# Ten of sixteen blocks of the first feed-forward by seven block products, and a list scheduler behind attention

## The chip, the cores and the metric

The kernel runs on one core of a Trainium2 chip. The metric is device time in microseconds of one execution; smaller is better. A profile is taken of one execution, and its own time is given beside the median of the runs.

## What is computed

Attention over 2 batches of 768 tokens with 8 heads of 64 (a band of near keys and 24 block summaries) gives `x` of 1536 tokens x 512. Then two feed-forwards follow, one behind the other:

```python
h = x @ w_in                      # 512 x 2048
y = (h - tanh(h)) @ w_out         # 2048 x 512
yn = y / sqrt(mean(y * y) + 1e-6) * rms_g
out = (silu(yn @ w_gate) * (yn @ w_val)) @ w_out2   # 512 x 1536 twice, 1536 x 512
```

The inputs are float32. Every operand of a feed-forward product is held as a high and a low part in the reduced format that TensorE multiplies at full rate, and one product is three matmuls: high x high, low x high, high x low.

## The kernel before

**Tiling.** The 1536 tokens are four groups of 384 (three tiles of 128); two groups are a half, `tp`. The columns of `w_in` come in 16 blocks of 128. One step of the first feed-forward (`steps`, L490 to L496) takes one block for one group: `up_mul` (L512) issues 4 x 3 matmuls of 384 columns into a PSUM bank `h`, ScalarE takes the tanh (L528), VectorE subtracts (L531), ScalarE and VectorE make the high and the low part (L536, L540), and three steps later (`LAG`) `down_mul` (L546) multiplies them with the block of `w_out`, nine matmuls of 512 columns. The blocks are done in four bundles (`NCH = [4, 3, 5, 4]`). Within a bundle the products of a token tile stay in one PSUM bank and are then copied or added to `part[t]` (`evac`, L561), so there are 4 x 12 evacuations.

**The second feed-forward** uses block products with fewer multiplications. For 256 columns of weight (`p`), half of the tokens, and the two halves of the 512 rows, the product is a 2 x 2 block product; `unit2` (L649) does it by seven products of sums and differences of blocks (Winograd's form of Strassen's method) instead of eight. A product is 2 x 3 matmuls of 384 columns (`product`, L639). The sums of weight blocks are made on GpSimd in `pair_of` (L225), those of token blocks in `operand` (L627). Intermediate sums build up in three banks `acc`, one `accx` and two `h`. `down2` (L713) then makes six token tiles, each in one of two banks `t2`, and VectorE adds each to `part`.

**The joint.** When a token group has its last part of the first feed-forward, `norm` (L593) takes squares, the inverse root and the scaling; `turn` (L614) transposes the scaled rows on TensorE; `operand` makes the parts.

**Weights** come as words of 64 bits, 512 KB a piece, through two or three buffers `raw`; ScalarE makes the signed part (L190), VectorE shifts and joins (L196, L197), and `split` (L200) makes the high part on ScalarE (L202) and the low part on GpSimd (L205). They lie in 13 slots used in a ring.

**Order.** Attention, with the first nine to twelve steps of the first feed-forward beside it, is issued in an order written out in `ORDER`, under a manual schedule. What stands behind it is issued in program order, with counters of rough time (`adv`, L792, `at`, L778) that say where decoding, norm and operands are put in, and the framework's own scheduler then orders the instructions of each engine by a simulated timeline.

Of the kernel before, what the change touches and what calls it, by code (L numbers as in the profile page):

```python
# [22 lines left out]
GT = 3  # L23
# [5 lines left out]
NCH = [4, 3, 5, 4]  # L29
NG = NT // GW  # L30
G0 = ((0, 3), (3, 3), (6, 3), (9, 3))
GN = tuple((GT * g, GT) for g in range(NG))
NP = FF2 // 256
SLOTS_A = 10
# [7 lines left out]
SB = 13  # L42
# [3 lines left out]
TS0 = 6  # L46
UF = 2
DT0 = 3.5
DT1 = 2.5
DLD = 10  # L50
DTR = 6
DPV = 10
DVL = 10
DEC = (1.8, 1.9)
TP0 = 1.2
TP1 = 1.0
TC = 0.6
TK01 = 1
TV = 4
TK1 = -8  # L60
TV1 = -8
TD0 = 11
DTD = 3.5
TM0 = 28
REST = 38
DM0 = 4
S2 = 2
EV = 4
PSV = 0
PTV = 0  # L70
KBUF = 4
PVS = (1, 1)
PB = 4
PTB = 3
SHIFT = {}
ALT = ()
OSA = 6
SSH = 8
TSEL = 0.3
TQ = (0.2, 3)  # L80
TVL = (6, 16)
ORD = [0, 2, 1, 3]
TKB = (4, 6)
VE = ((0, 1, 0, 0), (1, 1, 1, 1))
DTV = 0.25
# [25 lines left out]
TVS = 10  # L111
TCKW = {"schedule_with_timeline_sim": True}


@with_exitstack
def attn_moe_kernel(ctx: ExitStack, tc: tile.TileContext, ins, out, dbg=None):
# [39 lines left out]
    jobs = []  # L156
    m0 = 0
    for nch in NCH:
        jobs += [(name, m) for name in ("w_in", "w_out") for m in range(m0, m0 + nch)]
        m0 += nch  # L160
    for p in range(NP):
        jobs += [("w_gate", p), ("w_val", p), ("w_out2", 2 * p), ("w_out2", 2 * p + 1)]
    SLOTS_OF = {"w_in": 1, "w_out": 1, "w_gate": 4, "w_val": 3, "w_out2": 1}
    b2 = 2 * sum(NCH[:-2])
    b3 = b2 + 2 * NCH[-2]
    LENT = jobs[b2:b2 + 6] + jobs[b3 + NCH[-1]:b3 + NCH[-1] + 3]
    wt = {}
    nxt = {"job": 0, "slot": 0, "piece": 0}
# [8 lines left out]
    def room(n):  # L177
        while nxt["slot"] + n > free["n"]:
            yield "blocked"

    free = {"n": SLOTS_A, "t": 0.0, "gen": None, "at": 0.0}

    def load(name, m):
        raw = (state["raw"] if "raw" in state else rawp).tile([128, 1024], U32, name="raw")
        nc.sync.dma_start(out=raw, in_=ins[name][m].bitcast(U32))
        return raw.rearrange("p (n t) -> p n t", t=2)
# [5 lines left out]
    def words(r):  # L192
        a = dp.tile([128, 512], F32, name="da")
        t = dt_.tile([128, 512], U32, name="dt")
        signed(a, r)
        V.tensor_scalar(t, r[:, :, 0], 29, None, ALU.logical_shift_right)  # L196
        V.scalar_tensor_tensor(t, a.bitcast(U32), 3, t, ALU.logical_shift_left, ALU.bitwise_or)  # L197
        return t.bitcast(F32)

    def split(hi, lo, d, eng):  # L200
        if eng is A:
            A.activation(hi, d, AF.Copy)  # L202
        else:
            eng.tensor_copy(hi, d)
        G.tensor_tensor(lo, d, f(hi), ALU.subtract)  # L205

    def one(name, m):
        i = nxt["piece"]
        nxt["piece"] += 1
        r = load(name, m)  # L210
        yield
        d = words(r)
        yield
        if (name, m) in LENT:
            k = LENT.index((name, m))
            if k % 3 == 0:
                state["wx"] = state["xp"].tile([128, GT, 2, KD, 128], F32R, name="x2").rearrange("p a b c d -> p a b (c d)")
            w = state["wx"][:, k % 3]
        else:
            yield from room(1)  # L220
            w = slot()
        split(w[:, 0], w[:, 1], d, V if (i < EV) != (f"ev{i}" in ALT) else A)
        wt[name, m] = w

    def pair_of(name, p):  # L225
        r = load(name, 2 * p)
        yield
        d1 = words(r)
        r = load(name, 2 * p + 1)
        yield  # L230
        yield from room(1)
        wa = slot()
        split(wa[:, 0], wa[:, 1], d1, A)
        yield
        d2 = words(r)
        yield
        a11, a12, a21, a22 = d1[:, 0:256], d1[:, 256:512], d2[:, 0:256], d2[:, 256:512]
        sf = state["sf"].tile([128, 4, 256], F32, name="sf")
        G.tensor_tensor(sf[:, 0], a21, a22, ALU.add)
        G.tensor_tensor(sf[:, 1], sf[:, 0], a11, ALU.subtract)  # L240
        G.tensor_tensor(sf[:, 2], a11, a21, ALU.subtract)
        G.tensor_tensor(sf[:, 3], a12, sf[:, 1], ALU.subtract)
        yield from room(2)
        wb, wc = (slot().rearrange("p h (q c) -> p h q c", q=2) for _ in range(2))
        yield
        split(wb[:, 0, 0], wb[:, 1, 0], a22, A)
        yield
        split(wb[:, 0, 1], wb[:, 1, 1], sf[:, 0], A)
        yield
        split(wc[:, 0], wc[:, 1], sf[:, 1:3], A)  # L250
        if name == "w_gate":
            yield from room(1)
            wt["s4", p] = slot().rearrange("p h (q c) -> p h q c", q=2)
        q4 = 0 if name == "w_gate" else 1
        wd = wt["s4", p]
        split(wd[:, 0, q4], wd[:, 1, q4], sf[:, 3], A)
        wa = wa.rearrange("p h (q c) -> p h q c", q=2)
        wt[name, p] = {1: wa[:, :, 0], 2: wa[:, :, 1], 3: wd[:, :, q4], 4: wb[:, :, 0], 5: wb[:, :, 1], 6: wc[:, :, 0], 7: wc[:, :, 1]}

    def decode(name, m):  # L260
        return (pair_of if name in ("w_gate", "w_val") else one)(name, m)

    dec = {}

    def w_load(i):
        dec[i] = {"r": load(*jobs[i])}
        nxt["job"] = i + 1
        nxt["piece"] = i + 1
# [34 lines left out]
    kwin, kmax, vsum, vt_, last = {}, {}, {}, {}, {}  # L303
# [186 lines left out]
    steps = []  # L490
    m0 = 0
    for j, nch in enumerate(NCH):
        for g in GN if j else G0:
            for m in range(m0, m0 + nch):
                steps.append((j, g, m, m == m0, m == m0 + nch - 1))
        m0 += nch  # L496
    acc, part, gs = {}, {}, {}

    def triple(o, wh, wl, xh, xl, start, stop, **kw):
        T.matmul(o, wh, xh, start=start, stop=False, **kw)  # L500
        T.matmul(o, wl, xh, start=False, stop=False, **kw)  # L501
        last["PE"] = T.matmul(o, wh, xl, start=False, stop=stop, **kw)  # L502

    def down(o, w, g, j, first, end):
        js = slice(j * 128, (j + 1) * 128)
        T.matmul(o, g[:, 0, js], w[:, 0], start=first, stop=False)  # L506
        T.matmul(o, g[:, 1, js], w[:, 0], start=False, stop=False)  # L507
        last["PE"] = T.matmul(o, g[:, 0, js], w[:, 1], start=False, stop=end)  # L508
# [3 lines left out]
    def up_mul(i):  # L512
        _, g, m, _, _ = steps[i]
# [11 lines left out]
    def up_tanh(i):  # L525
        h, n = up_h[i]
        t = up_t[i] = tmp()[:, 0:n]
        A.activation(t, h, AF.Tanh)  # L528
# [4 lines left out]
    def up_high(i):  # L533
        t = up_t[i]
        gg = gs[i] = gp.tile([128, 2, GW], F32R, name="g")[:, :, 0:t.shape[-1]]
        last["ACT"] = A.activation(gg[:, 0], t, AF.Copy)  # L536

    def up_low(i):
        gg = gs[i]
        last["DVE"] = V.tensor_tensor(gg[:, 1], up_t.pop(i), f(gg[:, 0]), ALU.subtract)  # L540

    def up_step(i):
        for piece in (up_mul, up_tanh, up_less, up_high, up_low):
            piece(i)

    def down_mul(i, t):  # L546
        j, g, m, first, end = steps[i]
# [6 lines left out]
    def down_step(i):  # L554
        j, g, m, first, end = steps[i]
        for t in range(g[0], g[0] + g[1]):
            down_mul(i, t)
            if end:
                evac(acc.pop(t), t, j == 0)

    def evac(a, t, first, act=False):  # L561
        if first:
            part[t] = pp.tile([128, DM], F32, name="part") if t < 6 else state["pp"].tile([128, DM], F32, name="part2")
            if act or t % 3 == 1:
                A.activation(part[t], a, AF.Copy)  # L565
            else:
                V.tensor_copy(part[t], a)
        else:
            V.tensor_tensor(part[t], a, part[t], ALU.add)  # L569

    def squares(g, v):
        for j in range(GT):
            jk = state["jk"].tile([128, 512], mybir.dt.bfloat16, name="jk")
            A.activation(jk, part[g * GT + j], AF.Square, scale=DM ** -0.5, accum_out=v[:, j:j + 1])

    def inverse(g, v, y):
        r = sp.tile([128, GT], F32, name="rt")
        V.tensor_scalar(v, v, 1e-6, None, ALU.add)
        V.tensor_scalar(r.bitcast(U32), v.bitcast(U32), 1, None, ALU.logical_shift_right)
        V.tensor_scalar(y.bitcast(I32), r.bitcast(I32), -1.0, float(0x5F3759DF), ALU.mult, ALU.add)  # L580
        for _ in range(3):
            V.scalar_tensor_tensor(r, y, -0.5, y, ALU.mult, ALU.mult)
            V.tensor_tensor(r, r, v, ALU.mult)
            V.scalar_tensor_tensor(y, r, 1.5, y, ALU.add, ALU.mult)

    def scaled(g, y, j):
        x = part[g * GT + j]
        if SCE[g][j]:
            A.activation(x, x, AF.Copy, scale=y[:, j:j + 1])
        else:  # L590
            V.tensor_scalar(x, x, y[:, j:j + 1], None, ALU.mult)

# [364 lines left out]
```

## Time and profile before

| What | us |
|---|---|
| median of 3 runs (lowest, highest) | 635.87 (635.28, 636.94) |
| the profiled execution | 637.51 |
| its span, first to last instruction | 635.6 |
| TensorE busy in the span | 610.5 (96%) |
| VectorE | 392.3 (62%) |
| ScalarE | 324.0 (51%) |
| GpSimd | 227.1 (36%) |

Busy times are the union of an engine's instructions. Matmuls are pipelined, so each lasts about twice the distance from one to the next; distances from start to start are what they cost. "PEclk" is the clock granted to TensorE as a share of its full 2.4 GHz. Engines are named PE (TensorE), DVE (VectorE), ACT (ScalarE), POOL (GpSimd) and SP (the queue that issues DMAs); L and a number is a line of the kernel.

### The profile page before, as it was taken

To read this page: it belongs to the slowest core of one execution; us is meant where nothing else is said; L and a number is where in the kernel's file an instruction comes from. 1 tells how busy PE (TensorE), PEld (TensorE's weight loads), DVE (VectorE), ACT (ScalarE), POOL (GpSimd) and SP (SyncE) were. 2 spreads that over 40 slices of the span, in tenths; PEclk is the share of its full clock that TensorE was granted. 3 is DMA by queue.
4 is the path that set the end of the run, shared out by engine and by line. 5 is a ranking of instruction groups with operands and counts; after the bars stand their busy time and mean duration, and the time that the engine had idled before them with its cause. 6 is when DMAs were issued, how large, how long until landed. Compare 5 with 4: busy or idle time off the path is not lost.

```text
span 635.6 us, 9649 instructions
## 1 busy us (share of the span) xinstructions
PE 610.5 (96%) x3528; PEld 556.8 (88%) x3528; DVE 392.3 (62%) x897; ACT 324.0 (51%) x798; POOL 227.1 (36%) x237
## 2 busy tenths in 40 slices
PE   3889999999999999999999889999999999999997
PEld 3779988898989899999998879999999999999995
DVE  3788672455657545545568694765657656657544
ACT  1996984444444444434546575644454363453420
POOL 0666831122222222540000145663555355365300
PEclk9899999999999999999999899999999999999999
DMA  8898710312223222201000020301212122121013
GB/s 331 265 342 244 240 53 26 133 67 100 100 100 121 78 100 100 88 15 65 0 1 1 34 67 1 131 36 66 68 67 72 61 94 72 45 90 34 1 66 133
DMA packets 19640, 58.91 MB, mean 93 GB/s; under 512 B 2168, under 2 KB 5496, under 8 KB 19592
## 3 DMA queue, kind: packets, MB, share of 16 engines
q1 hardware_dynamic: 19592, 58.29, 27.0%
q8 instruction: 28, 0.46, 0.3%
q14 instruction: 20, 0.16, 0.1%
HBM read 54.84 MB, written 3.15 MB: 91 GB/s over the span
## 4 chain that ended last, share of the span: by engine, by line
PE 87%; ACT 5%; DMA 3%; DVE 3%; POOL 1%; issue 1%; SPq 0%; POOLq 0%
PE h L502 8%; PE h L500 8%; PE h L501 8%; PE acc L506 7%; PE acc L508 7%; PE acc L507 7%; PE t L506 5%; PE t L507 5%; PE t L508 5%; PE acc L500 5%; PE acc L502 5%; PE acc L501 5%; PE accx L502 3%; PE accx L501 3%; PE accx L500 3%; ACT P L441 2%
## 5 line engine op out<-in xcount | busy, mean ns | idle before, releaser
L205 POOL TENSOR_TENSOR w<-dt,w 128x512 fp32r<-128x512 f32 (+1 forms) x51 | 63.6, 1247 | 143.9 <-ACT w L202 113.5
L528 ACT ACTIVATE s<-h 128x384 f32<-128x384 f32 x64 | 31.2, 489 | 85.8 <-PE h L502 85.7
L531 DVE TENSOR_TENSOR s<-h,s 128x384 f32<-128x384 f32 x64 | 35.5, 555 | 63.4 <-ACT s L528 62.8
L569 DVE TENSOR_TENSOR part<-t,part 128x512 f32<-128x512 f32 x60 | 40.8, 688 | 41.4 <-PE t L508 40.9
L506 PE MATMUL t<-w,g 128*128 128x512 f32 x144 | 54.8, 395 | 2.8 <-ACT part L565 2.5
L507 PE MATMUL t<-w,g 128*128 128x512 f32 x144 | 56.9, 395 | 0.3 <-DVE g L659 0.3
L506 PE MATMUL acc<-w,g 128*128 128x512 f32 x144 | 57.1, 401 | 0.0
L508 PE MATMUL acc<-w,g 128*128 128x512 f32 x144 | 56.9, 395 | 0.0
L508 PE MATMUL t<-w,g 128*128 128x512 f32 x144 | 56.7, 394 | 0.0
L507 PE MATMUL acc<-w,g 128*128 128x512 f32 x144 | 56.7, 394 | 0.0
L540 DVE TENSOR_TENSOR g<-s,g 128x384 fp32r<-128x384 f32 x64 | 40.8, 640 | 24.0 <-ACT g L536 23.9
L197 DVE SCALAR_TENSOR_TENSOR dt<-da,dt 128x512 uint32<-128x512 uint32 x60 | 50.7, 846 | 5.8 <-ACT da L190 2.8
L501 PE MATMUL h<-x,w 128*128 128x384 f32 x148 | 50.1, 338 | 0.0
L500 PE MATMUL h<-x,w 128*128 128x384 f32 x148 | 49.8, 337 | 0.0
L502 PE MATMUL h<-x,w 128*128 128x384 f32 x148 | 49.7, 337 | 0.0
L658 ACT ACTIVATE g<-s 128x384 fp32r<-128x384 f32 x48 | 24.6, 520 | 49.3 <-POOL s L701 39.2
L536 ACT ACTIVATE g<-s 128x384 fp32r<-128x384 f32 x64 | 33.4, 523 | 30.5 <-DVE s L531 29.9
L659 DVE TENSOR_TENSOR g<-s,g 128x384 fp32r<-128x384 f32 x48 | 31.5, 667 | 24.1 <-ACT g L658 23.8
L190 ACT ACTIVATE da<-raw 128x512 f32<-128x512 f32 x68 | 44.7, 659 | 1.4 <-DMA raw<-w_out 1.3
L441 ACT ACTIVATE P<-P,nb 128x120 f32<-128x120 f32 x96 | 36.5, 384 | 15.3 <-DVE nb L435 15.1
L681 POOL TENSOR_TENSOR s<-s 128x384 f32<-128x384 f32 x12 | 12.2, 1019 | 88.0 <-DVE s L680 88.0
L500 PE MATMUL acc<-x,w 128*128 128x384 f32 x120 | 41.1, 343 | 1.5 <-ACT s L663 1.4
(164 smaller groups left out, 1703.8 us busy)
## 6 DMA issues: line engine op xcount, KB each, us to landing
raw<-w_out SPq DMA_DIRECT2D x28, 512.0 KB, 3.2
raw<-w_in SPq DMA_DIRECT2D x16, 512.0 KB, 4.9
q<-q SPq DMA_DIRECT2D x12, 512.0 KB, 8.9
raw<-w_gate SPq DMA_DIRECT2D x12, 512.0 KB, 3.2
raw<-w_val SPq DMA_DIRECT2D x12, 512.0 KB, 3.1
kw<-kw SPq DMA_DIRECT2D x8, 576.0 KB, 4.5
v<-vw SPq DMA_DIRECT2D x12, 384.0 KB, 5.0
out_dram<-part SPq DMA_DIRECT2D x12, 256.0 KB, 2.0
```

The costliest lines, as they stand in the source:

```text
L190: A.activation(a, r[:, :, 1].bitcast(F32), AF.Prelu, scale=2.0 ** -112, alpha=-(2.0 ** 32))
L197: V.scalar_tensor_tensor(t, a.bitcast(U32), 3, t, ALU.logical_shift_left, ALU.bitwise_or)
L205: G.tensor_tensor(lo, d, f(hi), ALU.subtract)
L441: A.activation(P[:, k], P[:, k], AF.Exp, scale=-1.0, bias=nb[:, k:k + 1], accum_out=sm[:, k:k + 1])
L500: T.matmul(o, wh, xh, start=start, stop=False, **kw)
L501: T.matmul(o, wl, xh, start=False, stop=False, **kw)
L502: last["PE"] = T.matmul(o, wh, xl, start=False, stop=stop, **kw)
L506: T.matmul(o, g[:, 0, js], w[:, 0], start=first, stop=False)
L507: T.matmul(o, g[:, 1, js], w[:, 0], start=False, stop=False)
L508: last["PE"] = T.matmul(o, g[:, 0, js], w[:, 1], start=False, stop=end)
L540: last["DVE"] = V.tensor_tensor(gg[:, 1], up_t.pop(i), f(gg[:, 0]), ALU.subtract)
L569: V.tensor_tensor(part[t], a, part[t], ALU.add)
```

## The change

Six blocks of `w_in` stay in the old form: four in `ORDER` and behind it, and two more, in two bundles. The other ten are five pairs of 256 columns, each done by `unit1`, seven products for each half of the tokens, in the order of `RUNS` (one pair for both halves; then two pairs for the first half and for the second, twice). Their weights are decoded by `pair_of`, now for `w_in` too, and need four slots a pair. The token operands are built from attention's output: `first_sum` adds high and low part, `operand` subtracts and splits; three of the seven use the old tiles as they are, one is written in place, three lie in new tiles. Each unit's six token tiles are multiplied with `w_out` by `down2` during the next unit, over two blocks each, and added to `part` on VectorE. `norm` and the transposes of the joint stand between units at written places. The load of the Silu table (`si`) is issued inside `ORDER`.

All work behind `ORDER` is first recorded as steps with an engine, a cost (time on the engine, latency, and whether it takes the access that VectorE and GpSimd share) and its readers and writers. `Plan.order` gives each step a due time, backwards from TensorE's written order, and places steps one by one, on each engine the one that can start first and, among equals, is due first. `Plan.issue` then issues everything in that order under the manual schedule. TensorE keeps the written order. In `unit2` the first two value products of block 0 come before the fifth gate product, and temporary tiles come from two pools (5 and 8 tiles) in place of one of 13.

```diff
-NCH = [4, 3, 5, 4]
+NCH0 = 4
+NCH1 = 2
+N0 = (NCH0 + NCH1) // 2
+NF = FF1 // 256 - N0
+RUNS = (1, 2, 2)
+FSG = ((0, 0), (1, 1))
+TNE = (('DVE', 'ACT'), ('ACT', 'DVE'))
+START = {"PE": 0.0, "DVE": 1.6, "ACT": 0.0, "POOL": -12.0, "SP": -1.0}
+C_T3, C_D3, C_TURN = (0.524, 0.69, 0), (0.695, 0.86, 0), (0.36, 0.52, 0)
+C_SIGN, C_SHIFT, C_JOIN = (0.56, 0.66, 0), (0.335, 0.416, 1), (0.6, 0.69, 1)
+C_G512, C_G256, C_G384, C_V384 = (1.25, 1.3, 1), (0.67, 0.72, 1), (0.98, 1.02, 1), (0.467, 0.551, 1)
+C_P384, C_P384A, C_E512, C_E512A = (0.467, 0.55, 0), (0.39, 0.49, 0), (0.6, 0.69, 0), (0.48, 0.58, 0)
...
+    def order(self, free):
...
+        while len(start) < len(S):
+            best = None
+            for e, L in line.items():
+                if e == "PE":
+                    L = [i for i in L if at < len(pe) and i == pe[at]]
+                for i in L:
+                    s = max(free[e], ready[i], lock if S[i][1][2] else -1e9)
+                    k = (s, due[i], i)
+                    if best is None or k < best[0]:
+                        best = k, i
...
+            start[i], done[i] = s, s + lat
+            free[e] = s + occ
+            if locks:
+                lock = s + occ
...
+    ctx.enter_context(tc.manual_schedule())
+    for key in ORDER:
+        tasks[key]()
...
+    def unit1(p, tp, fill, odd):
+        w = wt["w_in2", p]
+        ga, gb, gc = (Buf(q) for q in (("accx", "h", "h") if odd else ("acc",) * 3))
...
+        def shrink(s, row, half, ps=None):
+            t, x = Buf("s"), ps or s
+            v = lambda: x.tile[:, 0:GW]
+            act(AF.Tanh, lambda: t.tile, v, [x], [t])
+            if ps:
+                both("DVE", C_P384, lambda: t.tile, v, lambda: t.tile, ALU.subtract, [x], [t])
+            else:
+                both("POOL", C_G384, lambda: t.tile, v, lambda: t.tile, ALU.subtract, [x], [t])
+            g[row, half] = widen(t)
+
+        product(ga, w, tp, 1, True)
+        s11 = taken(ga)
+        product(gb, w, tp, 2, True)
+        added(s11, gb)
+        product(gc, w, tp, 5, True)
+        s22 = taken(gc)
+        product(ga, w, tp, 6, False)
+        s12 = taken(ga)
+        shrink(s11, 0, 0)
+        fill(0)
+        product(ga, w, tp, 7, False)
+        added(s22, ga)
+        shrink(s22, 1, 1)
+        fill(1)
+        product(gc, w, tp, 3, False)
+        added(s12, gc)
+        shrink(s12, 0, 1)
+        fill(2)
+        product(ga, w, tp, 4, False)
+        shrink(None, 1, 0, ga)
+        fill(3)
+        return g
...
+    def first_sum(tp, kk, kh, half):
+        d = xs[tp, kk, kh, half] = Buf("xs")
+        r, x = plain(tp, half, kh, kk)
+        eng = "POOL" if (kh, half) in FSG else "DVE"
+        both(eng, C_G384 if eng == "POOL" else C_V384, lambda: d.tile.rearrange("p (t n) -> p t n", t=GT), lambda: f(x(0)), lambda: f(x(1)), ALU.add, r, [d])
...
+    units, p0 = [], N0
+    for n in RUNS:
+        units += [("w_out", p, tp) for tp in range(2) for p in range(p0, p0 + n)]
+        p0 += n
+    units += [("w_out2", p, tp) for p in range(NP) for tp in range(2)]
+    last_p = N0 + NF - 1
...
+    for n, (name, p, tp) in enumerate(units):
+        if (name, p, tp) == ("w_out2", 0, 1):
+            turned(1, 1)
+            downs(prev, range(6))
+            prev = None
+
+        def fill(k, prev=prev):
+            if n == 0:
+                if k < 3:
+                    down_step(rest[k])
+            elif prev is None:
+                pass
+            elif prev[:2] == ("w_out", last_p):
+                if prev[2]:
+                    if k == 0:
+                        downs(prev, range(6))
+                    elif k == 1:
+                        turned(1, 0)
+                elif k < 2:
+                    downs(prev, range(3 * k, 3 * k + 3))
+            elif k < 3:
+                downs(prev, range(2 * k, 2 * k + 2))
+            if (name, p, tp) == ("w_out", last_p, 1) and k >= TAT:
+                turned(0, k - TAT)
...
+    plan.issue(dict(START))
```

In the diff, `taken` is a copy from PSUM on ScalarE, `added` an addition from PSUM on VectorE, `widen` the high part on ScalarE and the low part on VectorE, `both` an instruction with two inputs, and `turned` the four transposes of a token group, their copies and the operands made of them.

## Rows read from the trace of the kernel before

**Rows 1.** Busy time by stretches: engines, granted clock, DMA share.
```profile
core 0: us, PE busy (x) PEld busy (x) DVE busy (x) ACT busy (x) POOL busy (x), PEclk, DMA share, GB/s
116.70:349.50 232.80, 232.80 (x1179) 210.77 (x1179) 139.64 (x283) 108.98 (x219) 50.52 (x43) 1.00 0.21 73
349.50:384.00 34.50, 29.52 (x151) 26.34 (x150) 25.32 (x48) 22.11 (x48) 11.78 (x10) 0.95 0.13 47
384.00:624.00 240.00, 240.00 (x1250) 223.29 (x1248) 148.63 (x244) 111.83 (x241) 113.34 (x116) 1.00 0.18 62
...
340.00:360.00 20.00, 17.93 (x91) 16.53 (x90) 14.81 (x47) 13.08 (x28) 1.02 (x1) 0.91 0.01 2
```

**Rows 2.** Order in time, TensorE, first feed-forward: start, duration, line, tiles.
```profile
206.38 0.39 PE L506 MATMUL acc<-w,g 128*128 128x512 f32 x1
...
208.46 0.34 PE L500 MATMUL h<-xf,x 128*128 128x384 f32 x1
...
210.58 0.39 PE L506 MATMUL acc<-w,g 128*128 128x512 f32 x1
```

**Rows 3.** Order in time, TensorE, the joint; brackets: idle before, releaser.
```profile
349.48 0.83 PE L619 MATMUL t<-sel,part 128*128 128x128 f32 x6
...
353.47 0.54 PE L500 MATMUL acc<-x,w 128*128 128x384 f32 x1 [1.42 <-ACT s L663]
...
357.24 0.34 PE L500 MATMUL acc<-xf,w 128*128 128x384 f32 x1
...
364.45 0.82 PE L619 MATMUL t<-sel,part 128*128 128x128 f32 x6
365.02 0.42 PE L502 MATMUL h<-x,w 128*128 128x384 f32 x1
...
378.76 0.34 PE L501 MATMUL h<-x,w 128*128 128x384 f32 x1
381.63 0.50 PE L506 MATMUL t<-w,g 128*128 128x512 f32 x1 [2.52 <-ACT part L565]
```

**Rows 4.** Order in time, ScalarE, the joint: table load, first square, last scalings.
```profile
344.69 1.28 ACT L856 ACT_TABLE_LOAD   x1
...
346.10 0.61 ACT L574 ACTIVATE jk<-part 128x512 bf16<-128x512 f32 x1
...
351.32 1.32 ACT L589 ACTIVATE part<-part,ry 128x512 f32<-128x512 f32 x2
```

**Rows 5.** Groups by line and shape: count, busy us, mean ns, idle before.
```profile
L205 POOL TENSOR_TENSOR w<-dt,w 128x512 fp32r<-128x512 f32 x39 | 52.8, 1354 | 141.3 <-ACT w L202 110.9 <-DVE g L540 30.4
L540 DVE TENSOR_TENSOR g<-s,g 128x384 fp32r<-128x384 f32 x64 | 40.8, 640 | 24.0 <-ACT g L536 23.9
L531 DVE TENSOR_TENSOR s<-h,s 128x384 f32<-128x384 f32 x64 | 35.5, 555 | 63.4 <-ACT s L528 62.8
L528 ACT ACTIVATE s<-h 128x384 f32<-128x384 f32 x64 | 31.2, 489 | 85.8 <-PE h L502 85.7
L569 DVE TENSOR_TENSOR part<-acc,part 128x512 f32<-128x512 f32 x36 | 23.7, 683 | 4.9 <-PE acc L508 4.9
L681 POOL TENSOR_TENSOR s<-s 128x384 f32<-128x384 f32 x12 | 12.2, 1019 | 88.0 <-DVE s L680 88.0
```

**Rows 6.** Order in time, VectorE, then GpSimd, first feed-forward.
```profile
163.14 0.41 DVE L196 TENSOR_SCALAR dt<-raw 128x512 uint32<-128x512 uint32 x1
163.66 0.69 DVE L197 SCALAR_TENSOR_TENSOR dt<-da,dt 128x512 uint32<-128x512 uint32 x1
...
165.59 0.56 DVE L540 TENSOR_TENSOR g<-s,g 128x384 fp32r<-128x384 f32 x1 [0.59 <-ACT g L536]
...
166.68 1.50 DVE L197 SCALAR_TENSOR_TENSOR dt<-da,dt 128x512 uint32<-128x512 uint32 x1 [0.19 <-ACT da L190]
...
166.16 1.48 POOL L205 TENSOR_TENSOR x<-dt,x 128x512 fp32r<-128x512 f32 x1 [3.35 <-DVE g L540]
```

More of the change, by code (lines that the diff above doesn't have):

```diff
@@ L41 @@
 GB = 6
-SB = 13
+SB = 5
 PSH = 2
@@ L175, in slot @@
         return state["wp"].tile([128, 2, 512], F32R, name="w2")
[L177 to L181, printed above, removed]
     def load(name, m):
-        raw = (state["raw"] if "raw" in state else rawp).tile([128, 1024], U32, name="raw")
+        raw = rawp.tile([128, 1024], U32, name="raw")
         nc.sync.dma_start(out=raw, in_=ins[name][m].bitcast(U32))
@@ L207, in one @@
[L207 to L223, printed above, removed]
@@ L586, in scaled @@
[L586 to L591, printed above, removed]
-    def norm(g, t):
-        v = sp.tile([128, GT], F32, name="rv")
-        y = sp.tile([128, GT], F32, name="ry")
-        squares(g, v)
-        at(t + (3, 3, 1, 1)[g], lambda: inverse(g, v, y))
-        for j in range(GT):
-            at(t + (7, 7, 3, 4.6)[g] + 0.45 * j, lambda j=j: scaled(g, y, j))
@@ L792, in adv @@
[L792 to L802 removed]
+    task("si", lambda: A.activation(sp.tile([128, 1], F32, name="rv"), rg[:, 0:1], AF.Silu))
@@ L806, in need, with product @@
             while k not in wt:
-                if not work():
-                    raise RuntimeError(f"no slot for {k}")
-    def prepare(tp, half, t, dt):
+                name, m = next(todo)
+                (pair_of if name in ("w_in2", "w_gate", "w_val") else one)(name, m)
+    def product(o, w, tp, n, start):
+        rw, wv = w[n]
+        for kk in range(2):
+            x = xq[tp, n][kk]
+            step("PE", C_T3, lambda kk=kk, x=x: triple(o.tile[:, 0:GW], wv(0, kk), wv(1, kk), x[1](0), x[1](1), start and kk == 0, kk == 1, skip_group_check=True), [*rw, *x[0]], [o])
@@ new lines, in down2, with taken @@
+    def down2(name, p, tp, g, j):
+        t = 6 * tp + j
+        a = Buf("t")
+        for row in range(2):
+            lower(a, wt[name, 2 * p + row], g[row, j // 3], j % 3, row == 0, row == 1)
+        evac(a, t, (name, p) == ("w_out2", 0), tp == 0)
+        if (name, p) == ("w_out2", NP - 1):
+            x = P[t]
+            step("SP", C_STORE, lambda: nc.sync.dma_start(out=out[t * 128:(t + 1) * 128], in_=x.tile), [x])
+    def taken(a, pool="s", eng="ACT"):
+        s = Buf(pool)
+        copy(eng, C_P384A if eng == "ACT" else C_P384, lambda: s.tile, lambda: a.tile[:, 0:GW], [a], [s])
+        return s
@@ L887, in attn_moe_kernel, with opens @@
-    need(("w_out2", 2 * NP - 2), ("w_out2", 2 * NP - 1))
-    for j in range(6):
-        down2(*prev, j)
+        for kk in range(2):
+            for kh in range(2):
+                turn(tp, kk, kh, half)
+            for n in (5, 6, 7, 4, 3) if half else (1, 2):
+                operand(tp, kk, n)
+    att_ctx.close()
+    def opens(name, bufs, **kw):
+        return ctx.enter_context(tc.tile_pool(name=name, bufs=bufs, **kw))
+    state["wp"] = opens("wp2", SLOTS_B)
+    state["jk"] = opens("jk", 1)
@@ new lines, in down_step @@
+    def down_step(i):
+        g, m, first, end = steps[i]
+        need(("w_out", m))
+        w = wt["w_out", m]
+        for t in range(g[0], g[0] + g[1]):
+            if first:
+                accs[t] = Buf("acc")
+            lower(accs[t], w, ups[i], t - g[0], first, end)
+            if end:
+                evac(accs.pop(t), t, m < NCH0)
+    for i in range(n0, len(steps)):
+        up_step(i)
+        down_step(i - LAG)
+    rest = list(range(len(steps) - LAG, len(steps)))
+    units, p0 = [], N0
@@ new lines, in attn_moe_kernel, with downs @@
+    for n in RUNS:
[3 more added lines that the diff above has]
+    last_p = N0 + NF - 1
+    def downs(unit, js):
+        name, p, tp, g = unit
+        need((name, 2 * p), (name, 2 * p + 1))
+        for j in js:
+            down2(name, p, tp, g, j)
+            if (name, p) == ("w_out", last_p) and j % 3 == 2:
+                norm(2 * tp + j // 3)
+    for tp in range(2):
+        first_tiles(tp)
+        for kk in range(2):
+            for kh in range(2):
+                for half in range(2):
+                    first_sum(tp, kk, kh, half)
+            for n in (5, 6, 7, 4):
+                operand(tp, kk, n)
```

726 lines of the change are left out of this document (368 added, 358 removed), and 2 rows, old and new, of the table ORDER.

## The prediction

> **What bounds the kernel now.** I read the busy time by stretches first [rows 1]. From 116.7 us, where attention's last products are issued, to 349.5 us TensorE is busy for the whole 232.8 us, and from 384 to 624 us for the whole 240 us; the reader is to see that in the same rows VectorE is busy for 139.6 and 148.6 us, ScalarE for 109.0 and 111.8, GpSimd for 50.5 and 113.3. So both feed-forwards are bound by TensorE, with room of about 40% on the next engine. Only the joint between them, 349.5 to 384 us, has TensorE idle: 29.5 busy of 34.5 us. The order of TensorE's instructions in time [rows 3] then gives what the joint costs, start to start; the brackets at the line ends name what TensorE waited for, a ScalarE copy (L663, 1.42 us) and the first evacuation of `w_out2` (L565, 2.52 us):
>
> - The twelve transposes from 349.48 us take until 353.47, 3.99 us; six undisturbed ones take 0.57 (364.45 to 365.02), so twelve are worth 1.14 and 2.85 us are lost.
> - The next twelve products, 353.47 to 357.24 us, take 3.77 us. They run at half speed: the stretch 340 to 360 us is the one with a mean granted clock of 0.91 in [rows 1], so for some 3.5 us it is at the lower of its two levels, 1.2 GHz in place of 2.4, after TensorE had done little but transposes and waits for 4 us. At full speed they are 12 x 0.1767 = 2.12 us: 1.65 lost.
> - 378.76 to 381.63 us is 2.87 for one such product: 2.69 lost.
>
> Sum 7.2 us. Attention (before 116.7 us) keeps its written order but for one ScalarE instruction, so it keeps its time.
>
> **The change part by part.** *Seven products for eight.* Per pair of `w_in` blocks, the old form issues 2 blocks x 4 token groups x 4 x 3 = 96 matmuls of 384 columns (`up_mul`); the new `unit1` issues 7 products x 2 x 3 = 42 for each half of the tokens, 84 in all. Five pairs save 5 x 12 = 60. Twelve such matmuls take 208.46 to 210.58 us [rows 2], 0.1767 us each, where TensorE is full: 60 x 0.1767 = 10.6 us off the path. The products into `part` stay: 16 blocks x 12 tiles x 3 (nine take 206.38 to 208.46 us, 0.231 each). So do the transposes in the joint. From below: if every saved matmul left a wait of its own length it would be 0; above 10.6 the removed work can't give, since what is left streams as many columns as before.
>
> *What the other engines get for it.* A pair now takes 84 x 0.1767 + 72 x 0.231 = 31.5 us of TensorE. By [rows 5] VectorE has per unit three additions and one subtraction from PSUM (0.555 each) and four low parts (0.64), so 4.8, 9.6 a pair; twelve additions into `part` x 0.683 = 8.2, where the old order needed one per four blocks or so (84 evacuations in place of 48); four decoded pieces x (0.41 + 0.69) = 4.4 [rows 6]. Together 22.2 of 31.5 us, 70%, against 60% now. ScalarE has 22 instructions x 0.49 a pair where it had 16: 2.9 us more on 47% now [rows 1], under 60%. GpSimd: the 113.3 us of the second feed-forward [rows 1] over its 5.2 blocks of 46.3 us are 21.9 a block, less four multiplications of 1.02 and two splits of 1.354 leave 7.5 for decoding one pair into seven operands; a pair of the first then has 7.5 + 2.7 + 6 subtractions x 1.02 = 16.3 of 31.5 us, 52%. None is a bound; the second feed-forward runs TensorE full at 62% VectorE and 47% GpSimd. Weight loads are the same number on SP's queue with the same two buffers, at a DMA share of 0.2, each due one unit (14 us or more) after its slot frees: nothing; if one comes late TensorE waits for it in full.
>
> *The operands of the first feed-forward.* New are 16 sums of high and low parts (8 on VectorE, 8 on GpSimd) and 16 operands, each a subtraction, a high and a low part: 40 VectorE instructions with both inputs in SBUF and 16 copies on ScalarE. They lie beside the twelve remaining plain steps and the first two units, which give TensorE 12 x (12 x 0.1767 + 9 x 0.231) = 50.4, plus 13.7 and 15.7 us: 79.8 us of cover. Here is the tightest place. At 166.16 us GpSimd starts a 1.48 us subtraction; the VectorE join issued at 166.68 takes 1.50 us where the one at 163.66 took 0.69 [rows 6]: it stood until GpSimd was done. If all such pairs exclude each other, the 79.8 us must hold, on VectorE, 12 + 40 + 8 instructions of 0.56 and ten joins of 0.69, 40.5 us, and on GpSimd six splits (8.1), two pairs (15), 8 sums and 6 subtractions (14.3), 37.4 us: 77.9 in all. It just fits, with no reserve for anything that is ordered badly. The Trainium skill says the same more strictly (SBUF — State Buffer, "Who interferes with whom"): a VectorE instruction with two SBUF inputs and a GpSimd instruction that reads SBUF exclude each other for the whole instruction; by it no overlap at all is to be had here, and by the trace the one collision shown is a full block too. Bounds for the lateness: 0 if the order is good; 4.5 us if a wait like that at 349.48 us comes, with its half-speed stretch (2.85 + 1.65). I take 2, nearer to the waits without a fall of the clock.
>
> *The joint, written anew.* Between the norm of a token group and its transposes there now lie at least eight products (8.5 us), against 6.5 from the first square to the end of the last scaling now (346.10 to 352.64 us, [rows 4]), so the norm is hidden. What is late next is the first operand of the second feed-forward: the transposes (turned(0,0) and (0,1)) have one product between them and then four products, 4.2 us, while VectorE must copy four tiles, make four low parts and then two subtractions and low parts more, some 7 us, beside the low parts of the last unit. Bounds: 0, and the 7.2 us of now. I take 3.5, half of it: one wait of 2.7 us as at L565, and half of a half-speed stretch. The evacuations that TensorE waited 2.5 us for come at the same two banks, but ordered ahead of the operands by their due time.
>
> *The scheduler in the source.* TensorE's order is as written, the other engines' by list scheduling with costs; a wrong cost shows as a wait on an in-order engine, behind which all else on it stands. In the second feed-forward there is no wait to win (240 of 240), so this part is from 0 up; I leave it in the 2 + 3.5. *The Silu table* (1.28 us, [rows 4]) moves from 344.69 us into attention's end; if Tanh isn't in its set, it returns once or twice, on a ScalarE that is half idle: nothing.
>
> **Sum.** Against the profiled execution, 637.5 us (span 635.6): -10.6 - 7.2 + 2 + 3.5 = -12.3, so 625.2. It lies 1.6 above the median of the runs shown, 635.87; by that scale 623.5.
>
> **The rivals.** *Nothing new is late* (12%): the joint's 7.2 us go and none come; for it speaks the idle share of every other engine, against it the joint's VectorE work. 635.87 - 10.6 - 7.2 = 618.1.
>
> *Shared access of VectorE and GpSimd and the joint take it back* (20%): the 77.9 us that exclude each other don't fit, TensorE waits 4.5 us in the first units with a half-speed stretch, and the joint costs what it does now: 635.87 - 10.6 + 4.5 = 629.8. For it speaks [rows 6]; against it, that 240 us with 148.6 and 113.3 on the two engines held no TensorE wait.
>
> *Each unit waits: slower* (8%). Product 6 adds onto the bank of product 1, which ScalarE must have copied first; 12 matmuls, 2.1 us, are the cover, and one copy behind three others of 0.5 us eats it. The price of one such wait with its half-speed stretch is 4.5 us by [rows 3]. Of ten units, four times make 18, the whole gain of 17.8; with five, 635.87 - 17.8 + 22.5 = 640.6. Against it: the second feed-forward has the same pattern with the same cover and loses nothing.
>
> *It hardly comes to bear* (5%): two or three such waits beside an unchanged joint, 634 to 637.8.
>
> **How the numbers follow.** My forecast has 55%, on its own 619.5 to 626.5. 617.5 to 630.5 takes in nearly all of the first rival and two thirds of the second, leaving out 2 in 10. Faster by over 0.3% (1.9 us, about what a measurement of this kernel can tell from none) are the forecast and two rivals, 87%; within it 5%, slower 8%.
>
> **What would show it.** Right: 420 matmuls of 384 columns on the new products' line where 480 stood, at 0.177 us; TensorE full from 116.7 us to the joint but for a wait or two near the first units, named by an operand of VectorE; a joint of 2 to 5 us lost; VectorE near 70% in the block part. Wrong: a wait in every unit on the copies from the accumulators, a granted clock below 1 in more than two stretches, or a joint as long as now.

## The result, and the profile after

The changed kernel takes 631.0 us (629.28 to 632.36, six runs) against 636.36 for the kernel before (635.28 to 639.01, six runs): ratio 0.9911, interval 0.9886 to 0.9936. It is faster, by 5.4 us, where 12.3 were forecast, and lies 0.5 us above the range. The profiled execution is the shortest of the six, 629.28 us, span 627.5. The kernel before was profiled with a half-speed stretch at its joint (mean clock 0.995), the changed one without (1.00); between executions of equal mean clock, over all runs of the two kernels, the gain is 5.9 to 6.6 us (635.4 and 629.1 at 1.00, 636.7 and 630.8 at 0.997, 638.8 and 632.2 at 0.992).

The page of the changed kernel, busy time, share of the span and number of instructions by engine:

```profile
PE 598.8 (95%) x3468; PEld 542.7 (86%) x3468; DVE 452.5 (72%) x973; ACT 352.0 (56%) x859; POOL 295.6 (47%) x310
```

TensorE has 3468 matmuls where it had 3528: the 60 are gone. Its busy time fell by 11.7 us and the span by 8.1, so some of the gain was spent again. Busy time by stretches, with the columns of [rows 1]: plain steps and block units, the joint, the rest.

```profile
116.70:300.00 183.30, 183.13 (x914) 164.85 (x915) 154.98 (x251) 103.87 (x212) 100.75 (x96) 1.00 0.25 88
300.00:400.00 100.00, 92.22 (x478) 81.31 (x477) 81.25 (x183) 69.39 (x154) 42.22 (x43) 1.00 0.11 38
400.00:623.00 223.00, 222.81 (x1154) 206.46 (x1153) 141.30 (x223) 96.58 (x201) 98.40 (x99) 1.00 0.19 64
```

The block part is as full as the plain steps were, though VectorE now works 155.0 of 183.3 us (85%). The joint is where TensorE has its gaps, 7.8 us of 100 in busy time. TensorE's waits there, longest first, in the profiled execution: who waited for what, us in total, times, longest.

```profile
PE t L929 <- ACT xs L628: 2.5, 2, 2.1
PE accx L514 <- DVE xs L635: 1.6, 2, 0.8
...
PE t L929 <- DVE xs L630: 1.1, 2, 0.5
PE t L521 <- DVE g L635: 0.9, 2, 0.7
PE acc L514 <- ACT s L628: 0.7, 1, 0.7
```

L929 are the transposes, L514 to L516 the products, L520 to L522 the token tiles. In place of two large waits [rows 3] there are some ten smaller ones: transposes that wait for a bank's copy, and products that wait until a bank has been read before they add to it.

A wait alone tells too little, since the pipeline starts up again and the clock can fall. So the joint is measured as in the prediction: from start to start, less 0.175 us for a matmul of 384 columns, 0.231 for 512 and 0.095 for a transpose, summed over all of them; the sums are good to some 0.3 us. Between 300 and 400 us of the span this loss is 9.2 us before and 12.3 after; between 115 and 300 us it is 0.7 and 1.2, behind 400 us 1.1 and 0.1. The 9.2 has a half-speed stretch in it, the 12.3 has none.

### The profile page after: what moved, and what is told of

Its sections match the earlier page's. It is cut to its first block, busy times and chain, and to the rows that moved or that the text cites. A ratio compares the mean times of both kernels' runs of the same rounds, so it can differ in the third digit from the quotient of the medians.

```text
span 627.5 us, 9802 instructions
## 1 busy us (share of the span) xinstructions
PE 598.8 (95%) x3468; PEld 542.7 (86%) x3468; DVE 452.5 (72%) x973; ACT 352.0 (56%) x859; POOL 295.6 (47%) x310
## 4 chain that ended last, share of the span: by engine, by line
PE 77%; DVE 12%; ACT 7%; issue 1%; DMA 1%; SPq 0%; POOL 0%; DVEq 0%; POOLq 0%
PE t L521 8%; PE t L522 8%; PE t L520 8%; PE acc L514 6%; PE acc L516 6%; PE acc L515 6%; PE h L516 4%; PE h L514 4%; PE h L515 4%; PE accx L514 3%; PE accx L515 3%; PE accx L516 3%; ACT P L460 3%; PE acc L520 3%; PE acc L522 3%; PE acc L521 3%
## 5 line engine op out<-in xcount | busy, mean ns | idle before, releaser
L635 DVE TENSOR_TENSOR part<-t,part 128x512 f32<-128x512 f32 x120 | 82.2, 687 | 47.6 <-PE t L522 47.4
L521 PE MATMUL t<-w,g 128*128 128x512 f32 x264 | 103.9, 394 | 0.9 <-DVE g L635 0.9
L520 PE MATMUL t<-w,g 128*128 128x512 f32 x264 | 103.9, 394 | 0.6 <-DVE xs L630 0.4
L522 PE MATMUL t<-w,g 128*128 128x512 f32 x264 | 103.6, 392 | 0.0
L635 POOL TENSOR_TENSOR s<-s,xs 128x384 f32<-128x384 f32 x24 | 24.5, 1021 | 89.4 <-DVE xs L635 89.2
L514 PE MATMUL acc<-x,w 128*128 128x384 f32 x174 | 58.9, 339 | 0.7 <-ACT s L628 0.7
L520 PEld LDWEIGHTS t<-w,g 128*128 128x128 f32 x264 | 49.6, 188 | 11.6 <-DVE part L635 1.7
L522 PEld LDWEIGHTS t<-w,g 128*128 128x128 f32 x264 | 49.6, 188 | 10.9
L516 PE MATMUL acc<-x,w 128*128 128x384 f32 x174 | 58.7, 337 | 0.2 <-DVE x L635 0.2
L515 PE MATMUL acc<-x,w 128*128 128x384 f32 x174 | 58.5, 336 | 0.0
L521 PEld LDWEIGHTS t<-w,g 128*128 128x128 f32 x264 | 49.6, 188 | 10.2 <-DVE g L635 1.8
L635 POOL TENSOR_TENSOR w<-sf,w 128x256 fp32r<-128x256 f32 (+1 forms) x51 | 49.4, 981 | 12.4 <-ACT w L628 12.4
L740 ACT ACTIVATE s<-s 128x384 f32<-128x384 f32 x66 | 34.5, 522 | 33.6 <-DVE s L635 33.3
L635 POOL TENSOR_TENSOR s<-s 128x384 f32<-128x384 f32 x30 | 32.6, 1087 | 36.7 <-ACT s L740 34.6
L635 DVE TENSOR_TENSOR s<-acc,s 128x384 f32<-128x384 f32 x56 | 30.9, 552 | 25.1 <-PE acc L516 23.5
L628 ACT ACTIVATE w<-dt 128x512 fp32r<-128x512 f32 (+1 forms) x60 | 33.3, 565 | 12.0 <-DVE dt L646 11.4
```

The costliest lines, as they stand in the source:

```text
L628: step(eng, cost, (lambda: A.activation(o(), x(), AF.Copy)) if scale is None else (lambda: A.activation(o(), x(), AF.Copy, scale=scale())) ...
L635: step(eng, cost, lambda: ENG[eng].tensor_tensor(o(), x(), y(), op), r, w)
L740: step("ACT", C_A384, lambda: A.activation(o(), x(), fn), r, w)
```

## The experiments

Each ratio is to the kernel before on the same chip, beside its interval. "Loss" is the sum just described.

**The changed kernel again**, unaltered.

> The changed kernel once more, unaltered. Joint theory (the saved matmuls give their 10.6 us, and the joint of the two feed-forwards takes part of it back): about 631 us, 5 to 6 us under the kernel before, and 10 us or more of TensorE's time lost between 300 and 400 us of the span, again at the transposes and at the first products of the second feed-forward. Spread theory (the block part itself runs slower than its count of matmuls): losses of several us between 115 and 300 us. Whether a half-speed stretch follows the joint may differ from run to run; if it does, it adds 1.5 to 3 us.

Measured 631.1 us, ratio 0.9896 (0.9874 to 0.9919). Loss 1.2 us from 115 to 300 us, 14.9 in the joint: 2.6 more than in the first profile. The difference is a half-speed stretch. The stretch of the joint where it lies (columns as in [rows 1]):

```profile
340.00:360.00 20.00, 17.10 (x80) 15.03 (x79) 14.54 (x45) 14.90 (x33) 4.59 (x4) 0.83 0.18 55
```

and TensorE's instructions in order of time there (start, duration, line, idle before):

```profile
348.45 0.82 PE L929 MATMUL t<-sel,part 128*128 128x128 f32 x6
351.40 1.02 PE L929 MATMUL t<-sel,part 128*128 128x128 f32 x6 [2.14 <-ACT xs L628]
...
353.04 0.52 PE L514 MATMUL accx<-xf,w 128*128 128x384 f32 x1
353.36 0.52 PE L515 MATMUL accx<-xf,w 128*128 128x384 f32 x1
353.68 0.52 PE L516 MATMUL accx<-xf,w 128*128 128x384 f32 x1
```

Six transposes, 2.1 us of nothing, six more, and the products behind them come every 0.32 us in place of 0.175: 1.2 GHz for 2.4, granted clock 0.83 in this stretch. The first profile had the same wait (2.09) and a clock of 1.00 there. Who made the transposes wait is seen on the three other engines, ScalarE, VectorE and GpSimd, in the same execution:

```profile
343.61 1.34 ACT L628 ACTIVATE part<-part,ry 128x512 f32<-128x512 f32 x2 [1.46 <-DVE ry L912]
...
347.60 0.49 ACT L740 ACTIVATE s<-acc 128x384 f32<-128x384 f32 x1
349.55 1.33 ACT L628 ACTIVATE part<-part,ry 128x512 f32<-128x512 f32 x2 [1.46 <-DVE ry L912]
350.79 1.03 ACT L628 ACTIVATE xs<-t,rg 128x384 f32<-128x384 f32 x2
...
346.36 0.99 DVE L905 TENSOR_SCALAR rv<-rv 128x3 f32<-128x3 f32 x1
...
349.36 0.16 DVE L912 SCALAR_TENSOR_TENSOR ry<-rt,ry 128x3 f32<-128x3 f32 x1
...
346.24 1.08 POOL L635 TENSOR_TENSOR s<-s,xs 128x384 f32<-128x384 f32 x1 [19.40 <-DVE xs L635]
```

ScalarE was ready at 348.1, and the first three transposes, issued from 348.45 on, were done by about 348.8. But next in ScalarE's order are the last two scalings of `part`, and they wait until VectorE ends the inverse root at 349.5. That took from 346.36 to 349.52 us, 3.2 us; the plan has four steps of 0.46, 1.84. Its twelve small instructions follow each other every 0.2 us, and the first (0.99 us; 0.17 elsewhere) stood until GpSimd's multiplication of 346.24 was done. The token group that is being transposed had its own scalings at 343.61, in time; those at 349.55 are the next group's.

**Three pairs of blocks by seven products**, not five.

```diff
-NCH1 = 2
+NCH1 = 6
-RUNS = (1, 2, 2)
+RUNS = (1, 2)
```

> Three pairs of blocks by seven products in place of five (ten of the sixteen blocks plain). Joint theory: two pairs give back 2 x 12 matmuls x 0.1767 = 4.2 us, so the time is 4.2 us over the changed kernel (635.2 if that is 631.0), with the joint as it was. Spread theory: under 2 us over it, or none, since a block pair would then cost about what a plain pair costs.

Measured 635.0 us, ratio 0.9966 (0.9952 to 0.9980): 3.9 us over the changed kernel by the medians, 4.5 by the ratios, with 4.2 worked out. Loss 1.0 us before 300 us, 14.0 in the joint. A pair is worth its 12 matmuls.

**No joint.**

```diff
-            if (name, p) == ("w_out", last_p) and j % 3 == 2:
-                norm(2 * tp + j // 3)
-            turned(1, 1)
-                    elif k == 1:
-                        turned(1, 0)
-                turned(0, k - TAT)
```

> Leaves out the norm, the transposes and the operands of the second feed-forward, which multiplies with the first one's operands. Joint theory: the 12.2 us that TensorE loses at the joint and the 4.6 us of its 48 transposes go: 631 - 16.8 = 614.2 us, and TensorE has no loss over 1 us from 120 us to the end. Spread theory: 5 to 9 us off only, with losses left between 120 and 400 us.

Measured 616.3 us, ratio 0.967 (0.9647 to 0.9694): 14.9 us off, 16.8 expected. Loss 1.3 us before 300 us, 3.9 left in the stretch of the joint. So most of the lost time hangs on norm, transposes and operands; what is left is three waits of some 1 us in the first block of the second feed-forward, where products add to a bank that has just been written. They are there without norm and transposes too; in TensorE's waits of this run:

```profile
PE accx L514 <- DVE xs L635: 1.8, 2, 1.1
...
PE acc L514 <- ACT s L628: 0.6, 1, 0.6
```

**All blocks plain, ordered by the scheduler.** Four bundles of four blocks; the transposes of the first half stand between the last plain steps, five steps behind their group.

```diff
-    steps += [(g, m, m == NCH0, m == 2 * N0 - 1) for g in G0 for m in range(NCH0, 2 * N0)]
+    steps += [(g, m, m == m0, m == m0 + 3) for m0 in range(NCH0, 2 * N0, 4) for g in G0 for m in range(m0, m0 + 4)]
...
+        if (i - len(steps)) in TURNS:
+            turned(0, TURNS.index(i - len(steps)))
```

> All sixteen blocks plain, in four bundles of four, everything behind attention ordered by the scheduler in the source; the transposes of the first half stand between the last plain steps. Joint theory with the blame on what the block form puts beside the joint: 60 matmuls more than the changed kernel (+10.6 us), and a joint of 4 us or less in place of 12.2: 631 + 10.6 - 8 = 633.6 us, under the kernel before. Rival, the scheduler's own order is what costs at the joint, whatever stands beside it: 631 + 10.6 = 641.6 us, 5 us over the kernel before.

Measured 639.9 us, ratio 1.004 (1.0026 to 1.0054): slower than the kernel before, which does the same products in the old order. Loss in the joint 13.2 us. This is nearer to the rival (641.6) than to the first theory (633.6): with no block product beside it, the joint of the new order still costs 3 to 4 us more (2.7 by the medians, 4.0 by the loss), and the block form then gives 8.7. How much of that is the scheduler's and how much the written order of TensorE, which `unit2` shares with the changed kernel, this run doesn't tell.

**The norm's planned cost** as the trace has it.

```diff
-C_SQ, C_N3 = (0.72, 0.82, 0), (0.46, 0.46, 1)
+C_SQ, C_N3 = (0.72, 0.82, 0), (0.6, 0.75, 1)
```

> The changed kernel with one planned cost set to what the trace shows: a step of the inverse root 0.6 us on VectorE (0.46 planned). Queue theory (the 2.4 us at the third transposes, and the half-speed stretch of 2.5 us behind it, come from the last scalings, which ScalarE was given ahead of the transposes' copies and which waited for a later inverse root than planned): that wait goes and with it most of the half-speed stretch: 3 to 5 us faster than the changed kernel, about 627. Load theory (VectorE has more work in the joint than TensorE can wait for, in whatever order): within 1 us of the changed kernel.

Measured 627.4 us, ratio 0.9839 (0.9822 to 0.9856): 3.7 us faster than the changed kernel. ScalarE in order of time at the same place:

```profile
349.28 1.05 ACT L628 ACTIVATE xs<-t,rg 128x384 f32<-128x384 f32 x2 [0.59 <-PE t L929]
...
350.75 1.33 ACT L628 ACTIVATE part<-part,ry 128x512 f32<-128x512 f32 x2
```

The copies now stand ahead of the scalings and wait for the transposes, as they should. The inverse root itself is no shorter (345.68 to 348.97 us, with other work between its steps); only the order changed. The wait of 2.1 us is 0.3, in TensorE's order in time,

```profile
349.92 1.02 PE L929 MATMUL t<-sel,part 128*128 128x128 f32 x6 [0.34 <-ACT xs L628]
```

the clock is 1.00 there, the joint's loss 10.4.

**Products swapped** in the first block of the second feed-forward.

```diff
+        if p == 0:
+            product(vc, wv, tp, 5, True)
+            v22 = taken(vc, "xs")
         product(ga, w, tp, 7, False)
...
+        for last in ((1, 0) if p == 0 else (0, 1)):
+            if last:
+                product(vc, wv, tp, 3, False)
...
+            else:
+                product(va, wv, tp, 4, False)
...
```

> In the two units of the first block of the second feed-forward, where no token tiles stand between the products, the fifth value product stands ahead of the seventh gate product, and the third value product ahead of the fourth. Cover theory (three waits of 0.9 to 1.0 us, each on a copy or an addition that must read a bank before the next product adds to it, now with a product of 1.06 us between): 2.5 to 3 us faster, about 628.5, and those three waits gone. Load theory: the waits move to the next operand, under 1 us faster.

Measured 626.7 us, ratio 0.9827 (0.981 to 0.9844): 4.5 us faster. TensorE's waits from the third on (the first two are attention's):

```profile
PE t L936 <- ACT xs L628: 1.8, 2, 1.3
PE t L936 <- DVE xs L630: 1.4, 2, 0.8
PE t L521 <- DVE g L635: 1.3, 3, 0.7
```

No product waits for an addition or a copy from its bank any more; loss 9.8 us. The half-speed stretch isn't in this trace either, which makes it more than the three waits.

**Four banks for the first transposes.**

```diff
-        ps, d = Buf("t"), Buf("xs")
+        ps, d = Buf("h" if tp == 0 and kh else "t"), Buf("xs")
```

> The transposes of the first half of the tokens take two more PSUM banks (the two called h, free then), four in place of two. Bank theory (the 2.4 us lost at them come from waiting for a bank's copy): 2 us faster, about 629, losses at the first two groups of transposes gone. Load theory: the transposes no longer wait, but the products behind them wait as much longer for their operands: within 0.7 us of the changed kernel.

Measured 627.6 us, ratio 0.9858 (0.9835 to 0.9881), whose interval just overlaps that of the changed kernel: 2.4 us faster by the ratios, 3.5 by the medians. The first two groups of transposes have no wait left in the trace; a new wait of 0.4 us for an operand stands behind them. The execution profiled is one with a half-speed stretch (629.85 us, granted clock 0.83 from 340 to 360 us), behind the wait on ScalarE's queue, which is still there (2.2 us). The clock's part shows here among single executions: three with a mean clock of 0.997 to 1.0 take 627.2, 627.5 and 627.6 us, two with 0.994 and 0.992 take 629.9 and 631.0. Against 627.5 us, the middle one of the three, the half-speed stretch is 2.3 to 3.5 us.

**Transposes of the first half earlier**, by two places.

```diff
-TAT = 2
+TAT = 0
...
-            if (name, p, tp) == ("w_out", last_p, 1) and k >= TAT:
+            if (name, p, tp) == ("w_out", last_p, 1) and k in (TAT, TAT + 1):
```

> The transposes of the first half stand two places earlier in the last block unit (8 us or so of products and tiles more between them and the second feed-forward). Cover theory (the joint wants time between transposes and operands): the waits at the transposes and first operands of the first half, 3.5 us together, fall to 1: 2 to 3 us faster. Load theory: VectorE, busy for 18 of 20 us there, is late by as much with the tiles of the block part: within 1 us, or slower.

Measured 634.4 us, ratio 0.995 (0.9934 to 0.9966): 3.3 us slower, a miss for the cover theory. The stretch of the transposes, columns as in [rows 1], and then two of TensorE's waits:

```profile
320.00:340.00 20.00, 17.94 (x94) 15.68 (x92) 19.54 (x35) 13.57 (x30) 9.68 (x10) 1.00 0.01 1
```

```profile
PE t L520 <- DVE xs L630: 2.0, 2, 1.8
PE t L520 <- DVE part L635: 1.8, 1, 1.8
```

VectorE is busy 19.5 of 20 us. What it does for the transposes it doesn't do for the tiles (`part`), so TensorE waits 1.8 us for one of them, at 340.6 us. The other wait of 1.8 us is later, at 365.9, behind the transposes of the second half, and the wait on ScalarE's queue (2.5 us) is still there. Loss 16.4.

**The three edits together** (cost, swap, banks).

> The planned cost of the norm, the swapped products and the four banks together. If the waits at the joint are separate causes, the losses between 300 and 400 us fall from 14.9 us to about 6 without a half-speed stretch: the two single gains without the shared half-speed stretch, 2.4 + 2.7 + 2 for the banks, and 2.5 for the stretch: about 622.5 us. Load theory (VectorE's work fills the joint): not under 625.

Measured 624.3 us, ratio 0.9802 (0.9781 to 0.9823): the fastest here, 12.5 us under the kernel before and 6.9 under the changed one by the medians. Loss 7.7. A wait that was short grew; the joint, columns as in [rows 1], TensorE's longest wait in it, and VectorE, then GpSimd, in order of time just before its end:

```profile
300.00:400.00 100.00, 96.36 (x500) 86.93 (x500) 83.99 (x184) 69.50 (x156) 44.01 (x43) 0.98 0.12 38
```

```profile
PE acc L516 <- DVE x L635: 1.8, 1, 1.8
```

```profile
330.29 3.10 DVE L635 TENSOR_TENSOR xs<-xs 128x384 f32<-128x384 f32 x3
...
330.47 0.97 POOL L635 TENSOR_TENSOR w<-sf,w 128x256 fp32r<-128x256 f32 x1 [4.30 <-ACT w L628]
331.39 1.58 POOL L635 TENSOR_TENSOR w<-dt,w 128x512 fp32r<-128x512 f32 x1
```

At 332 us TensorE waits 1.8 us for the low part of an operand of the first half of the tokens, for gate product 6 of its first unit (0.2 us in the changed kernel). Three subtractions ahead of it on VectorE take 0.55, 1.09 and 1.62 us; the last two end 0.41 us after the GpSimd instructions beside them, which end at 331.44 and 332.98. In the changed kernel no GpSimd instruction lies there and each takes 0.55. The clock of 0.98 over the stretch shows a short fall behind the wait. The profiled execution is the longest of the four; the two with a mean clock of 1.00 take 623.5, so of the 1.8 us between the median and 622.5 some 0.8 is such a fall, and how much of the rest is this wait no run shows.

**Six pairs, with the three edits.**

```diff
-NCH1 = 2
+NCH1 = 0
-RUNS = (1, 2, 2)
+RUNS = (1, 1, 2, 2)
```

> With the three edits, six pairs of blocks by seven products, so no plain block behind attention's bundle, 33 us less cover for the first operands. Arithmetic alone: 2.1 us under the kernel with the three edits. If VectorE's two-input instructions and GpSimd's exclude each other, as in the prediction's sum of 77.9 us in 79.8, the operands come late: cover falls to some 46 us and the work to some 68, so 10 to 22 us of waits before 200 us, 8 to 20 us slower than it.

Measured 634.3 us, ratio 0.9957 (0.9941 to 0.9972): 10.0 us slower than with five pairs. Two stretches of the first units, and TensorE's two longest waits behind attention:

```profile
140.00:160.00 20.00, 14.62 (x60) 11.58 (x60) 18.57 (x31) 10.01 (x21) 9.46 (x8) 0.86 0.17 53
160.00:180.00 20.00, 17.43 (x77) 14.73 (x77) 15.79 (x27) 10.05 (x23) 10.94 (x11) 0.93 0.16 53
```

```profile
PE acc L516 <- DVE x L635: 5.4, 4, 1.9
PE acc L514 <- ACT s L628: 2.5, 1, 2.5
```

Of the four waits for `x` three lie here (3.6 us), the fourth (1.85 us) is the joint's. Loss 14.4 us from 115 to 200 us, against 0.5 with five pairs; it has waits for weights from GpSimd in it (1.7 us) and much time at half speed (0.86 and 0.93). The first operands are late as soon as the plain blocks that cover them go.

**All plain, cost and products mended.**

```diff
-C_SQ, C_N3 = (0.72, 0.82, 0), (0.46, 0.46, 1)
+C_SQ, C_N3 = (0.72, 0.82, 0), (0.6, 0.75, 1)
```

and the swap as above.

> All blocks plain, ordered by the scheduler, with the planned cost of the norm and the swapped products mended. If these two faults are what the scheduler cost there, 3 to 5 us under the all-plain run, 635 to 637, level with the kernel before; against the kernel with three edits it is 60 matmuls more, 10.6 us and the banks' 2. If the block form itself makes the joint dearer, the distance to the kernel with three edits is under 9 us.

Measured 635.6 us, ratio 0.9983 (0.9972 to 0.9995): 4.2 us under the all-plain run, level with the kernel before to 0.2%. Loss in the joint 8.4 us, against 13.2. The three edits with block products are 11.3 us under it: 60 matmuls, and whatever the banks give, which was not measured apart.

**Subtractions of the joint on GpSimd**, with the three edits.

```diff
+            e = "POOL" if state.get("joint") else "DVE"
-            both("DVE", C_V384, lambda: d.tile, lambda: a.tile, lambda: b.tile, ALU.subtract
+            both(e, C_G384 if e == "POOL" else C_V384, lambda: d.tile, lambda: a.tile, lambda: b.tile, ALU.subtract
```

> With the three edits, the 16 subtractions of the second feed-forward's operands on GpSimd (1.02 us each) in place of VectorE (0.47 from start to start). Load theory: 7.5 us less for VectorE where it is busiest, 1 to 3 us faster than the three edits alone. Exclusive-access theory: GpSimd's 16 us shut out VectorE's low parts meanwhile, 2 to 6 us slower.

Measured 634.7 us, ratio 0.9967 (0.9954 to 0.9980): 10.5 us slower, worse than either theory said. VectorE, then GpSimd, in order of time:

```profile
333.07 0.99 DVE L635 TENSOR_TENSOR x<-xs,x 128x384 fp32r<-128x384 f32 x1 [1.47 <-ACT x L628]
333.98 1.36 DVE L635 TENSOR_TENSOR g<-s,g 128x384 fp32r<-128x384 f32 x1
335.27 1.34 DVE L635 TENSOR_TENSOR x<-xs,x 128x384 fp32r<-128x384 f32 x1
...
331.68 4.52 POOL L635 TENSOR_TENSOR xs<-xs 128x384 f32<-128x384 f32 x4 [0.49 <-DVE x L635]
```

Low parts of 0.55 us take 1.0 to 1.4 while GpSimd works through its subtractions, and GpSimd's four take 4.5 in place of 4.1: the two engines take turns. Loss 16.6; part of it is half speed, with a clock of 0.88, 0.95 and 0.91 in the three stretches from 320 to 380 us. A GpSimd subtraction is also 0.55 us longer than VectorE's on the way to its operand, and this run doesn't tell the two causes apart.

## Why the prediction was wrong

The direction was right and the size was not. Its steps, one by one:

- *Seven products for eight, 10.6 us.* Right: 60 matmuls fewer; two pairs less cost 3.9 to 4.5 us (4.2 worked out); all plain against block products, both with cost and swap mended, is 11.3 us, the banks' part in it included.
- *No other engine a bound in the block part.* Right: the loss from 115 to 300 us is 1.2 us. VectorE was busier than worked out (70%): 85% of the stretch with the first operands in it, and 79% from 200 to 300 us, behind them.
- *First operands 2 us late.* Too high: 0.5 us more loss than before. That it just fits was right. VectorE is busy 19.6 of 20 us there, and with six pairs 14.4 us are lost. A collision, VectorE and then GpSimd, in the changed kernel:

```profile
142.20 1.64 DVE L635 TENSOR_TENSOR x<-xs,x 128x384 fp32r<-128x384 f32 x1
...
141.76 1.67 POOL L635 TENSOR_TENSOR w<-sf,w 128x512 fp32r<-128x512 f32 x1 [0.37 <-ACT w L628]
```

and the stretch it lies in, columns as in [rows 1]:

```profile
140.00:160.00 20.00, 20.00 (x102) 18.09 (x101) 19.61 (x30) 9.07 (x20) 10.85 (x10) 1.00 0.00 1
```

  The low part takes 1.64 us, 1.2 of them until GpSimd ends at 143.43. The Trainium skill (SBUF — State Buffer, "Who interferes with whom") says that a VectorE instruction with two SBUF inputs contends with a GpSimd instruction that reads SBUF; the trace agrees, 1.64 us for 0.55.
- *The joint, 3.5 us in place of 7.2.* This step failed. The joint costs 12.3 us in the shortest execution and 14.9 with its half-speed stretch, against 9.2 before by the same account, its half-speed stretch included; the 7.2 were the three largest places of these 9.2. The sentence "so the norm is hidden" was the weak one: it counted the eight products between a token group's norm and that group's transposes. In the second half, only five products (5.3 us) lie between the second group's norm and the first group's transposes, and that norm's last scalings stand on ScalarE's queue ahead of the copies of these transposes, behind an inverse root of 3.2 us. The prediction had looked for the late step on VectorE's operands, where the wait was 0.2 us (with the three edits it is 1.8). The second cause was not looked for: in the two units of block 0 no token tiles lie between the products, at three places, so a product adds to a bank right behind the product before it, where it has two tiles of cover elsewhere. The third, two banks for twelve transposes in a row, stood in the code. Each was taken away by itself: 3.7, 4.5 and 2.4 to 3.5 us, in which the changed kernel's half-speed stretch goes too, wholly or in part. Between executions with a mean clock of 0.999 or 1.000, two or three of each kernel, it is 2.0, 2.6 and 1.8 us, (6.4 in sum) and 5.6 for the three together, so the causes are nearly separate.
- *The scheduler from 0 up, inside the 2 + 3.5.* Too low: all plain blocks in the new order are 0.4% slower than in the old one, and 0.2% faster with the planned cost and the order of the products mended; the second of these is a fault of TensorE's written order and not the scheduler's.

With the measured sizes, from two executions that both have a half-speed stretch (the kernel before, and the changed kernel again), the sum is -10.6 + 0.5 + (14.9 - 9.2) - 1.0 behind 400 us = -5.4. The spans of these two changed by -6.0 (635.6 and 629.6), the medians by -5.4: the account holds to some 0.6 us, and that it meets the medians is chance. Of the rivals the second came near the outcome (629.8) with half of the right cause: the joint took it back, the shared access in the first units did not. The Silu table shows in no wait of TensorE, with two table loads in all as before.

What stays open: what the wait of 1.8 us with the three edits costs, whose cause the trace shows as a collision with GpSimd; an order that would mend it was not tried. Nor did a run separate shared access from the longer subtraction on GpSimd.

## What to carry to other kernels

A saved matmul is worth its distance from start to start only as long as every in-order queue at the next joint keeps up, so walk each queue there, ScalarE's too, and ask what stands ahead of the instruction that TensorE waits for. A list scheduler is as good as its costs: compare each planned cost with the trace, the chains of tiny instructions above all. Between two products that add to one bank there has to be other TensorE work as long as the read between them.

## What the runs showed of the hardware

- Tiny VectorE instructions (128 x 3) follow each other every 0.2 us in the inverse root, and one of them stood 0.99 us for 0.17 beside a GpSimd instruction.
- A wait of 2.1 us among transposes was followed by a half-speed stretch (granted clock 0.83 from 340 to 360 us) in one profiled execution and not in another of the same kernel; among five executions with four banks it costs 2.3 to 3.5 us of 630.
- A product that adds to a bank whose last product has just ended and is still to be read by VectorE or ScalarE costs 0.9 to 1.0 us, at three places of the changed kernel.
- VectorE instructions with two inputs in SBUF, 0.55 us each elsewhere, take 1.0 to 1.6 us beside a GpSimd instruction in the cases shown, and end about 0.4 us after it.
